# Decode attention, two blocks: the last output row in four column groups instead of two

## The chip, the cores and the metric

The kernel runs on one core of one Trainium2 chip. The metric is device time in microseconds for one execution, as the median of several runs. A profiled execution gives a trace beside it; its span is the time from the first to the last instruction, and lies about a microsecond below the measured time of a run.

## What is computed

Two independent attention blocks, A and B, each with one query token. A looks at the last 2048 positions of its key and value caches, B at all 8192. The two output rows of 576 values are concatenated.

```python
def block(x, k_cache, v_cache, wq, wo, W):        # A: W = 2048, B: W = 8192
    q = (x @ wq).reshape(1, 1, 32, 128).transpose(0, 2, 1, 3)
    k = jnp.repeat(k_cache[:, :, 8192 - W:, :], 2, axis=1)
    v = jnp.repeat(v_cache[:, :, 8192 - W:, :], 2, axis=1)
    p = softmax(jnp.einsum("bhqd,bhkd->bhqk", q, k) * 128 ** -0.5)
    o = jnp.einsum("bhqk,bhkd->bhqd", p, v)
    return o.transpose(0, 2, 1, 3).reshape(1, 1, 4096) @ wo      # wo: 4096 x 576
out = jnp.concatenate([block(A), block(B)], axis=-1)             # 1 x 1 x 1152, bf16
```

Everything is bf16. 102.76 MB are read from memory, nearly all of it the caches of 16 heads, wq and wo, each used once.

## The kernel before

The program is written as five lists of operations, one for each engine, in the order in which they are to run (`Prog`, L37). `op` adds an operation that tells the others by its engine's own semaphore; `load` adds one with a semaphore of its own (a DMA, or a copy whose end is counted with others). `deps` are names, which `emit` turns into waits. There is no scheduler: the order on each engine is the order in the source.

All loads are issued by SP in one order and go through a ring in SBUF of 72K bf16 values per partition (`place`, L167): wq of A and B, then K and V for units of four heads (four units of A, four of B), then wo of A in one piece and wo of B in five. `NWO` (L34) gives those pieces: A's 32 k at once, B's in 17, 8, 4, 2 and 1 k. One k is a slice of 128 rows of wo, 576 columns, spread over 128 partitions (147,456 bytes).

For each unit DVE transposes K in slabs (L350), PE makes scores (L367), ACT takes the exponent (L406), DVE transposes the probabilities, and PE multiplies by V (L431, four matmuls side by side in four strips of 32 columns of the array, each writing 32 partitions of a bank). The unit's result is copied out and folded (L438, L447). After the last unit the sums are inverted and the 32 heads' outputs are brought to the layout `oP`: partitions hold 128 rows of the contraction, and column k is the k-th slice (L482 to L499).

The output rows come last (L502 to L525). For each of the two blocks P and each k, two matmuls of one output row are made with `oP[:, P, k]` as weights: columns 0 to 319 (`N0` = 320) and columns 320 to 575. Both blocks use the bank `fb = qb[0]`. The four rows lie at partitions 0 and 32 (A) and 64 and 96 (B), that is, each in a strip of its own. The matmuls of one piece of wo are one operation, F*P.c*, that waits for that piece. F0.0 is A's, F1.0 to F1.4 are B's. When a block's last piece is done, ACT copies the 320 columns (L519) and DVE the 256 (L521) into one partition of `outsb`; both count on `s_row[P]`, and when it is 2, SP stores the row of 1152 bytes with one DMA (L523). SP's last operation waits until both stores have landed (`s_out` at 32).

Of the kernel before, what the change touches and what calls it, by code (L numbers as in the profile page):

```python
# [4 lines left out]
BF16 = mybir.dt.bfloat16  # L5
# [3 lines left out]
ACT = mybir.ActivationFunctionType  # L9
# [5 lines left out]
DM = 576  # L15
# [5 lines left out]
NQ = G // 4  # L21
# [6 lines left out]
ZA = 128 + 24  # L28
BIG = 1e30
N0 = 320  # L30
RING = 72 * 1024
NSEM = 24
NKT = 3
NWO = [[32], [17, 8, 4, 2, 1]]  # L34


class Prog:  # L37
# [9 lines left out]
    def op(self, eng, fn, deps=(), name=None):  # L47
        self.ops[eng].append((fn, tuple(deps), name, None))
        if name is not None:
            assert name not in self.where, name  # L50
            self.where[name] = (eng, len(self.ops[eng]) - 1)

    def load(self, eng, fn, sem, value, deps=(), name=None, step=16):
        self.ops[eng].append((fn, tuple(deps), None, (sem, step)))
        if name is not None:
            assert name not in self.dma, name
            self.dma[name] = (sem, value)
# [40 lines left out]
def bass_concat_heads__sliding_block_cached__gqa_block_cached__decode_kernel(nc, A_x, A_k_cache, A_v_cache, A_wq, A_wo,  # L98
# [6 lines left out]

    ring = nc.alloc_sbuf_tensor("ring", [128, RING], BF16)
    ktb = nc.alloc_sbuf_tensor("ktb", [128, NKT * SLAB], BF16)
# [35 lines left out]
    oq = nc.alloc_sbuf_tensor("oq", [128, 2, HQ], BF16)  # L143
    oP = nc.alloc_sbuf_tensor("oP", [128, 2, HQ], BF16)
    warm = nc.alloc_sbuf_tensor("warm", [128, 8], F32)
    outsb = nc.alloc_sbuf_tensor("outsb", [1, 2 * DM], BF16)

    sb = [nc.alloc_psum_tensor("sb%d" % b, [128, 512], F32) for b in range(2)]
    qb = [nc.alloc_psum_tensor("qb%d" % b, [128, 512], F32) for b in range(2)]
# [4 lines left out]
    def view(t, free, offset, dims, parts=128, p0=0):  # L154
        return bass.AP(tensor=t, offset=p0 * free + offset, ap=[[free, parts], *dims])

    pg = Prog(nc)
    op, load = pg.op, pg.load
    s_x = [nc.alloc_semaphore("s_x%d" % i) for i in range(2)]
    s_ld = [nc.alloc_semaphore("s_ld%d" % i) for i in range(NSEM)]  # L160
    s_out = nc.alloc_semaphore("s_out")
    s_row = [nc.alloc_semaphore("s_row%d" % i) for i in range(2)]
# [4 lines left out]
    def place(size, uses, issue, name):  # L167
        if at[0] + size > RING:
            at[0] = 0
        lo, hi = at[0], at[0] + size  # L170
        at[0] = hi
        deps = []
        for r in list(live):
            if r[0] < hi and lo < r[1]:
                deps += r[2]
                live.remove(r)
        n = nload[0]
        nload[0] += 1
        if n >= NSEM:
            deps += uses_of[n - NSEM]  # L180
        uses_of.append(list(uses))
        live.append((lo, hi, list(uses)))
        t = ring[:, lo:hi]
        load("sp", lambda e: issue(e, t), s_ld[n % NSEM], 16 * (n // NSEM + 1), deps=deps, name=name)
        return t
# [39 lines left out]
    for P in range(2):  # L225
        k0 = 0
# [6 lines left out]
    def slab(kind, i, s):  # L233
# [10 lines left out]
       deps=["id0"], name="ident")  # L244
# [15 lines left out]
    for c in range(2):  # L260
        op("dve", lambda e, c=c: e.tensor_reduce(par[:, c:c + 1], view(identf, 128, c, [[2, 64]]), AX.X, ALU.add),
           deps=["identf"], name="par%d" % c)
# [3 lines left out]
    for P in range(2):  # L266
        op("dve", lambda e, P=P: e.tensor_copy(  # L267
            view(xdup, 256, 128 * P, [[2, 64], [1, 2]], parts=1),
            view(xrow, 2 * DM, P * DM + 512, [[1, 64], [0, 2]], parts=1)), deps=["x%d" % P], name="xd%d" % P)
        for k in range(5):  # L270
            def mm(e, P=P, k=k):
                if k < 4:
                    lhsT = view(xrow, 2 * DM, P * DM + k, [[4, 128]], parts=1)
                else:
                    lhsT = xdup[0:1, P, :]
                return e.matmul(banks[2 * P + k // 4][:, (k % 4) * 128:(k % 4 + 1) * 128], lhsT=lhsT,  # L276
                                rhs=onesb[0:1, :], start=True, stop=True)
            op("pe", mm, deps=["x%d" % P, "onesb", "xd%d" % P], name="xT%d.%d" % (P, k))
        op("dve", lambda e, P=P: e.tensor_copy(
            xrep[:, P, 0:4, :].rearrange("p k m -> p (k m)"), banks[2 * P][:, :]), deps=["xT%d.3" % P], name="xr%d.0" % P)  # L280
        for c in range(2):
            op("dve", lambda e, P=P, c=c: e.tensor_scalar(
                xrep[:, P, 4 + c, :], banks[2 * P + 1][:, 0:128], par[:, c:c + 1], None, ALU.mult),
                deps=["xT%d.4" % P, "par%d" % c], name="xr%d.%d" % (P, 1 + c))
# [3 lines left out]
       deps=["identf"], name="clsb")  # L288
    op("dve", lambda e: e.tensor_reduce(clsa[:], view(identf, 128, 0, [[1, 8], [8, 16]]), AX.X, ALU.add),
       deps=["identf"], name="clsa")  # L290
    op("dve", lambda e: e.tensor_reduce(sel[:], view(identf, 128, 0, [[1, 32], [32, 4]]), AX.X, ALU.add),
       deps=["identf"], name="sel")
# [6 lines left out]
    for P in range(2):  # L299
        for n in range(8):  # L300
            u = 8 * P + n
            bank = banks[u % 4]

            def mm(e, P=P, n=n, bank=bank):
                for k in range(5):
                    if k < 4:
                        lhsT, o = xrep[:, P, k, :], wq_at[P, 0][:, k * w + n * 512:k * w + (n + 1) * 512]
                    else:
                        lhsT, o = xrep[:, P, 4 + n // 4, :], wq_at[P, 1][:, (n % 4) * 512:(n % 4 + 1) * 512]
                    ins = e.matmul(bank[:, :], lhsT=lhsT, rhs=o, start=(k == 0), stop=(k == 4))  # L310
                return ins
            op("pe", mm, deps=["wq%d.0" % P, "wq%d.1" % P] + XR + (["qe%d" % (u - 4)] if u >= 4 else []),
               name="qmm%d.%d" % (P, n))
            op("act", lambda e, u=u, bank=bank: e.activation(qsb[:, u % 4, :], bank[:, :], ACT.Copy),  # L314
               deps=["qmm%d.%d" % (P, n)] + (["qT%d" % (u // 2 - 2)] if u >= 4 else []), name="qe%d" % u)
            if n % 2:
                op("dve", lambda e, u=u, n=n: e.transpose(  # L317
                    ktb[:, (n - 1) * 512:(n + 1) * 512].bitcast(I32),
                    qsb[:, u % 4 - 1:u % 4 + 1, :].rearrange("p a n -> p (a n)").bitcast(I32)),
                    deps=["qe%d" % (u - 1), "qe%d" % u] + (["z0.%d" % i for i in range(4)] if P else []),  # L320
                    name="qT%d" % (u // 2))
        for b in range(4):
            if P == 1:
# [3 lines left out]
                    deps=["qT%d" % u for u in range(4, 8)] + ["zb0"], name="z1.%d" % b)  # L327
            else:
# [3 lines left out]
                    deps=["qT%d" % u for u in range(4)] + ["za0"], name="z0.%d" % b)  # L332
# [4 lines left out]
    k0 = [sum(nslab[:i]) for i in range(NU)]  # L337
# [117 lines left out]
    for i in range(NU):  # L455
        n = nslab[i + 1] if i + 1 < NU else 0
# [33 lines left out]
       deps=["lsel", "lselA", "nb%d" % last, "mr%d" % last], name="L")  # L490
# [3 lines left out]
        deps=["rl", "O%d" % last], name="on")  # L494
    op("dve", lambda e: e.transpose(oq[:].rearrange("p c k -> p (c k)"), on[:].rearrange("p c k -> p (c k)")),
       deps=["on"], name="oq")
# [2 lines left out]
    op("dve", lambda e: e.tensor_copy(oP[:].rearrange("p c k -> p (c k)"), mb[:, 64:128]), deps=["pm"], name="oP")  # L499


    fb = qb[0]  # L502
    for P in range(2):
        k0 = 0
        for c, kk in enumerate(NWO[P]):
            def mm(e, P=P, c=c, k0=k0, kk=kk):
                for k in range(kk):
                    for n in range(2):
                        r, lo, hi = 32 * (2 * P + n), n * N0, N0 + n * (DM - N0)
                        ins = e.matmul(fb[r:r + 1, 0:hi - lo], lhsT=oP[:, P, k0 + k:k0 + k + 1],  # L510
                                       rhs=wo_at[P, c][:, k * DM + lo:k * DM + hi],
                                       start=(k0 + k == 0), stop=(k0 + k == HQ - 1))
                return ins
            op("pe", mm, deps=["wo%d.%d" % (P, c), "oP", "exp%d" % (NQ - 2)], name="F%d.%d" % (P, c))
            k0 += kk
        done = "F%d.%d" % (P, len(NWO[P]) - 1)
        r, lo = 64 * P, P * DM

        load("act", lambda e, r=r, lo=lo: e.activation(outsb[0:1, lo:lo + N0], fb[r:r + 1, 0:N0], ACT.Copy),  # L519
             s_row[P], 2, deps=[done], name="f%d" % P, step=1)  # L520
        load("dve", lambda e, r=r, lo=lo: e.tensor_copy(outsb[0:1, lo + N0:lo + DM], fb[r + 32:r + 33, 0:DM - N0]),  # L521
             s_row[P], 2, deps=[done], step=1)
        load("sp", lambda e, lo=lo: e.dma_start(out[0, 0:1, lo:lo + DM], outsb[0:1, lo:lo + DM]),  # L523
             s_out, 16 * (P + 1), deps=["f%d" % P], name="out%d" % P)
    op("sp", None, deps=["out1"])  # L525

    pg.emit()
# [28 lines left out]
```

## Time and profile before

| | |
|---|---|
| time, median of 3 runs | 246.25 us (246.15 to 246.38) |
| profiled execution, span | 245.2 us |
| busy PE / DVE / ACT | 172.3 / 129.1 / 24.3 us |
| read from memory | 102.76 MB, 419 GB/s over the span |
| output matmuls (L510) | 128, busy 11.3 us, from 232.3 us on |
| weight loads of L510 | 128, 93 ns mean |
| copy of 320 columns (ACT L519) | 428 ns mean, two |
| copy of 256 columns (DVE L521) | 420 ns mean, two |
| stores (SP L523) | two of 1.1 KB, issued at 240.2 and 244.1 us |

Times in the trace are microseconds from the first instruction. Engines: PE is TensorE's matmul, PEld its weight load, which runs beside matmuls; DVE is VectorE, ACT ScalarE, SP the engine that issues the loads and stores here (its queue is SPq). A row of the timeline gives the start, the duration, what runs, its tiles (out<-in) with their shapes, and in brackets how long the engine had been idle and what ended that. The granted clock (PEclk) is the share of TensorE's full clock, in tenths in the 40 slices of the page and as a fraction in a table of stretches. The chain of waits goes back from the last instruction, at each step to what released it.

The page's DMA section counts, beside the kernel's loads, seven packets of 16 KB that carry instructions.

### The profile page before, as it was taken

How to read it: one execution, taken by the hardware profiler on the slowest of the kernel's cores; microseconds unless marked ns; L12 is line 12 of the kernel's file. 1: busy time of each engine (PE TensorE's matmuls, PEld its weight loads, DVE VectorE, ACT ScalarE, POOL GpSimd, SP SyncE). 2: the span in 40 equal slices, each digit the busy share in tenths (PEclk: the TensorE clock that was granted, in tenths of full speed). 3: DMA queues.
4: the chain of work that ended last, by engine and by line, in shares of the span. 5: the costliest groups of instructions: out<-in, count | busy, mean ns of one | idle time of the engine just before them, and what ended most of it. 6: DMA issues, size and time to landing. Idle time of an engine off the chain costs nothing.

```text
span 245.2 us, 2253 instructions
## 1 busy us (share of the span) xinstructions
PE 172.3 (70%) x960; PEld 71.8 (29%) x961; DVE 129.1 (53%) x162; ACT 24.3 (10%) x52; POOL 8.2 (3%) x15
## 2 busy tenths in 40 slices
PE   0269967787867994889582869945579939257197
PEld 0124422224433222432130523211423213213154
DVE  0422547667789986699501699810679920500201
ACT  2004540021201000100000100000010000200001
POOL 8400000000000000000000000000000000000000
PEclk9999995789999997569957578989657985677559
DMA  7999999999999999998999999999999999999994
GB/s 267 420 457 410 437 428 425 433 428 457 440 430 387 468 428 428 452 470 385 406 428 425 438 476 428 438 406 425 438 466 460 395 406 430 428 438 409 430 407 158
DMA packets 4481, 102.90 MB, mean 420 GB/s; under 512 B 500, under 2 KB 632, under 8 KB 1144
## 3 DMA queue, kind: packets, MB, share of 16 engines
q1 hardware_dynamic: 4468, 102.76, 97.9%
q8 instruction: 7, 0.11, 0.2%
q14 instruction: 2, 0.02, 0.0%
q10 hardware_dynamic: 4, 0.00, 0.0%
HBM read 102.76 MB, written 0.00 MB: 419 GB/s over the span
## 4 chain that ended last, share of the span: by engine, by line
DMA 55%; PE 29%; DVE 12%; ACT 2%; issue 2%; SPq 0%; DVEq 0%
DMA ring<-in_B_v_cache_dram 40%; DMA ring<-in_A_wo_dram 10%; DVE ktb L350 9%; PE vb L431 8%; DMA ring<-in_A_wq_dram 5%; PE qb L367 5%; PE qb L510 5%; PE sb L310 5%; PE qb L310 4%; ACT psb L406 1%; DVE pta L414 1%; PE ob L447 1%; PE sb L367 1%; PE qb L359 1%; PE mb L397 1%
## 5 line engine op out<-in xcount | busy, mean ns | idle before, releaser
L350 DVE STREAM_TRANSPOSE ktb<-ring 128x1024 int32<-128x1024 int32 x80 | 92.8, 1211 | 29.5 <-DMA ring<-in_B_k_cache_dram 28.3
L367 PE MATMUL sb<-ktb,zb 128*128 128x512 bf16 x256 | 76.0, 437 | 23.7 <-DVE ktb L350 21.1
L367 PEld LDWEIGHTS sb<-ktb,zb 128*128 128x128 bf16 x256 | 23.4, 106 | 72.4 <-DVE ktb L350 45.9
L431 PE MATMUL vb<-ring,pts 128*32 128x512 bf16 x256 | 24.7, 567 | 18.5 <-DMA ring<-in_B_v_cache_dram 14.4
L367 PE MATMUL qb<-ktb,za 128*128 128x512 bf16 x64 | 19.4, 449 | 2.8 <-DVE ktb L350 2.8
L431 PEld LDWEIGHTS vb<-ring,pts 128*32 128x32 bf16 x256 | 9.0, 134 | 33.6 <-DMA ring<-in_B_v_cache_dram 16.7
L438 ACT ACTIVATE xo<-vb 128x512 f32<-128x512 f32 x8 | 4.8, 597 | 129.4 <-PE vb L431 129.4
L418 DVE STREAM_TRANSPOSE pts<-psb 32x512 bf16<-32x512 bf16 x16 | 11.3, 703 | 9.5 <-ACT psb L406 9.3
L510 PE MATMUL qb<-ring,oP 128*1 128x256 bf16 (+1 forms) x128 | 11.3, 340 | 4.0 <-DMA ring<-in_A_wo_dram 4.0
L317 DVE STREAM_TRANSPOSE ktb<-qsb 128x512 int32<-128x512 int32 x8 | 5.7, 711 | 15.0 <-ACT qsb L314 15.0
L310 PE MATMUL sb<-ring,xrep 128*128 128x512 bf16 x40 | 11.4, 442 | 2.7 <-DMA ring<-in_A_wq_dram 2.7
L447 PEld LDWEIGHTS ob<-sel,xo 128*128 128x128 f32 x64 | 10.9, 244 | 3.8 <-ACT xo L438 2.2
L447 PE MATMUL ob<-sel,xo 128*128 128x8 f32 x64 | 10.1, 285 | 1.2 <-ACT xo L438 1.2
L367 PEld LDWEIGHTS qb<-ktb,za 128*128 128x128 bf16 x64 | 6.1, 109 | 13.4 <-issue 5.8
L310 PE MATMUL qb<-ring,xrep 128*128 128x512 bf16 x39 | 9.5, 393 | 0.0
L510 PEld LDWEIGHTS qb<-ring,oP 128*1 128x1 bf16 x128 | 7.0, 93 | 8.3 <-DMA ring<-in_A_wo_dram 4.1
L521 DVE CAST outsb<-qb 1x256 bf16<-1x256 f32 x2 | 0.8, 420 | 14.7 <-PE qb L510 14.7
L491 DVE RECIPROCAL rl<-mb 128x64 f32<-128x64 f32 x1 | 0.6, 558 | 12.3 <-PE mb L488 12.3
L276 PE MATMUL sb<-onesb,xrow 1*128 1x128 bf16 x4 | 0.6, 298 | 9.2 <-DVE xdup L267 9.2
L392 DVE TENSOR_REDUCE mr<-mb 1x8 f32<-1x128 f32 x8 | 1.9, 240 | 9.5 <-PE mb L384 9.5
L310 PEld LDWEIGHTS sb<-ring,xrep 128*128 128x128 bf16 x40 | 4.3, 109 | 8.6 <-issue 5.3
L314 ACT ACTIVATE qsb<-sb 128x512 bf16<-128x512 f32 x8 | 4.8, 597 | 19.1 <-PE sb L310 19.1
(65 smaller groups left out, 68.8 us busy)
## 6 DMA issues: line engine op xcount, KB each, us to landing
ring<-in_B_k_cache_dram SPq DMA_DIRECT2D x8, 4096.0 KB, 24.5
ring<-in_A_k_cache_dram SPq DMA_DIRECT2D x4, 2048.0 KB, 30.5
ring<-in_A_v_cache_dram SPq DMA_DIRECT2D x4, 2048.0 KB, 25.4
ring<-in_B_v_cache_dram SPq DMA_DIRECT2D x2, 4096.0 KB, 23.8
ring<-in_A_wo_dram SPq DMA_DIRECT2D x1, 4608.0 KB, 23.9
ring<-in_A_wq_dram SPq DMA_DIRECT2D x1, 4096.0 KB, 12.5
ring<-in_B_wq_dram SPq DMA_DIRECT2D x1, 4096.0 KB, 22.6
ring<-in_B_wo_dram SPq DMA_DIRECT2D x1, 2448.0 KB, 29.3
```

Of the source, the lines that this page charges most:

```text
L310: ins = e.matmul(bank[:, :], lhsT=lhsT, rhs=o, start=(k == 0), stop=(k == 4))
L314: op("act", lambda e, u=u, bank=bank: e.activation(qsb[:, u % 4, :], bank[:, :], ACT.Copy), deps=["qmm%d.%d" % (P, n)] + (["qT%d" % (u // ...
L317: op("dve", lambda e, u=u, n=n: e.transpose(ktb[:, (n - 1) * 512:(n + 1) * 512].bitcast(I32), qsb[:, u % 4 - 1:u % 4 + 1, :].rearrange("p ...
L350: op("dve", lambda e: e.transpose(kt.bitcast(I32), src.bitcast(I32)), deps=[landed] + (["S%d" % (k - NKT)] if k >= NKT else Z), name="T%d. ...
L359: e.matmul(bank[:, :], lhsT=mkl[:].rearrange("p a h r -> p (a h r)"), rhs=mkr[:].rearrange("p q h -> p (q h)"), start=True, stop=False)
L367: ins = e.matmul(bank[:, :], lhsT=lhsT, rhs=view(ktb, KT, (k % NKT) * SLAB + 64 * c + v, [[128, 16], [2, 32]]), start=(side == "B" and s = ...
L397: op("pe", lambda e: e.matmul(mb[:, 128:129], lhsT=mexp[0:1, :], rhs=onesf[0:1, 0:1], start=True, stop=True), deps=["mx%d" % i, "ones"], n ...
L418: op("dve", lambda e, b=b: e.transpose(view(pts, NB * 128, 2 * b, [[8, 16], [128, NB], [1, 2]], 32, 32 * b), psb[32 * b:32 * b + 32, :]), ...
L431: ins = e.matmul(vbank[i][32 * j:32 * j + 32, :], lhsT=lhsT, rhs=src[:, 512 * j:512 * j + 512], start=(s == 0), stop=(s == nslab[i] - 1))
L438: op("act", lambda e: e.activation(xo[:, c, :], vbank[i][:, :], ACT.Copy), deps=["V%d.%d" % (i, nslab[i] - 1)] + (["O%d" % (i - 1)] if i e ...
L447: ins = e.matmul(ob[:, at:at + 8], lhsT=xo[:, c, 128 * t:128 * t + 128], rhs=sel[:, 8 * t:8 * t + 8], start=(t == 0), stop=(t == 3))
L510: ins = e.matmul(fb[r:r + 1, 0:hi - lo], lhsT=oP[:, P, k0 + k:k0 + k + 1], rhs=wo_at[P, c][:, k * DM + lo:k * DM + hi], start=(k0 + k == 0 ...
```

## The change

A's row stays as it is: two column groups in `qb[0]`, copied into partition 0 of `outsb`, stored in one piece. B's row is computed in the other bank, `qb[1]`, in four groups of 144 columns at partitions 0, 32, 64 and 96. ACT copies partitions 0 to 32 (33 of them, of which the first and the last carry results) and DVE partitions 64 to 96, 144 columns each, into a new tile `outq` at the same partitions. One DMA stores four pieces of 288 bytes, from partitions 0, 32, 64 and 96. B's matmuls name the exponent of A's last unit (exp3) as a dependency, in place of exp2, since `qb[1]` held that unit's scores. The pieces of wo and their loads are unchanged.

```diff
+N1 = DM // 4
...
-    outsb = nc.alloc_sbuf_tensor("outsb", [1, 2 * DM], BF16)
+    outsb = nc.alloc_sbuf_tensor("outsb", [1, DM], BF16)
+    outq = nc.alloc_sbuf_tensor("outq", [128, N1], BF16)
...
-    fb = qb[0]
+    parts = [[(0, 0, N0), (32, N0, DM)], [(32 * j, N1 * j, N1 * j + N1) for j in range(4)]]
     for P in range(2):
-        k0 = 0
+        fb, k0 = qb[P], 0
         for c, kk in enumerate(NWO[P]):
-            def mm(e, P=P, c=c, k0=k0, kk=kk):
+            def mm(e, P=P, c=c, k0=k0, kk=kk, fb=fb):
                 for k in range(kk):
-                    for n in range(2):
-                        r, lo, hi = 32 * (2 * P + n), n * N0, N0 + n * (DM - N0)
+                    for r, lo, hi in parts[P]:
                         ins = e.matmul(fb[r:r + 1, 0:hi - lo], lhsT=oP[:, P, k0 + k:k0 + k + 1],
                                        rhs=wo_at[P, c][:, k * DM + lo:k * DM + hi],
                                        start=(k0 + k == 0), stop=(k0 + k == HQ - 1))
                 return ins
-            op("pe", mm, deps=["wo%d.%d" % (P, c), "oP", "exp%d" % (NQ - 2)], name="F%d.%d" % (P, c))
+            op("pe", mm, deps=["wo%d.%d" % (P, c), "oP", "exp%d" % (NQ - 2 + P)], name="F%d.%d" % (P, c))
             k0 += kk
...
+        else:
+            load("act", lambda e: e.activation(outq[0:33, :], qb[1][0:33, 0:N1], ACT.Copy),
+                 s_row[P], 2, deps=done, name="f1", step=1)
+            load("dve", lambda e: e.tensor_copy(outq[64:97, :], qb[1][64:97, 0:N1]), s_row[P], 2, deps=done, step=1)
+            load("sp", lambda e: e.dma_start(
+                bass.AP(tensor=out.tensor, offset=out.offset + DM, ap=[[N1, 4], [1, N1]]),
+                bass.AP(tensor=outq, offset=0, ap=[[32 * N1, 4], [1, N1]])), s_out, 32, deps=["f1"], name="out1")
```

In the kernel after, the matmuls of both rows stand at line 511.

More of the change, by code (lines that the diff above doesn't have):

```diff
@@ L513, in mm @@
                 return ins
-            op("pe", mm, deps=["wo%d.%d" % (P, c), "oP", "exp%d" % (NQ - 2)], name="F%d.%d" % (P, c))
+            op("pe", mm, deps=["wo%d.%d" % (P, c), "oP", "exp%d" % (NQ - 2 + P)], name="F%d.%d" % (P, c))
             k0 += kk
[L516 to L524, printed above, removed]
+        done = ["F%d.%d" % (P, len(NWO[P]) - 1)]
+        if P == 0:
+            load("act", lambda e: e.activation(outsb[0:1, 0:N0], qb[0][0:1, 0:N0], ACT.Copy),
+                 s_row[P], 2, deps=done, name="f0", step=1)
+            load("dve", lambda e: e.tensor_copy(outsb[0:1, N0:DM], qb[0][32:33, 0:DM - N0]),
+                 s_row[P], 2, deps=done, step=1)
+            load("sp", lambda e: e.dma_start(out[0, 0:1, 0:DM], outsb[0:1, :]), s_out, 16, deps=["f0"], name="out0")
+        else:
[5 more added lines that the diff above has]
+                bass.AP(tensor=outq, offset=0, ap=[[32 * N1, 4], [1, N1]])), s_out, 32, deps=["f1"], name="out1")
     op("sp", None, deps=["out1"])
```

## The prediction

> **What bounds the kernel now.** First the page's slices: how busy the DMA engines are, and the clock that TensorE was granted.
>
> ```profile
> span 245.2 us, 2253 instructions
> ...
> PEclk9999995789999997569957578989657985677559
> DMA  7999999999999999998999999999999999999994
> ```
>
> The DMA engines are at 90% or more in nearly every slice but the last, so the end is set by when the last bytes of weights land, and by what follows them. Then the chain of waits, from 220 us on.
>
> ```profile
> 5 pieces in order of time: start us, us, what
> 208.37 23.91 DMA ring<-in_A_wo_dram
> 232.28 0.04 issue
> 232.32 11.31 PE qb L510 x94
> 243.63 0.02 issue
> 243.65 0.43 ACT outsb L519
> ```
>
> The chain names the output matmuls of L510 for 11.31 us, but it stops at the copy, and a chain of PE work doesn't say whether PE was waiting. The timeline of the last stretch does.
>
> ```profile
> 242.96 0.09 PEld L510 LDWEIGHTS qb<-ring,oP 128*1 128x1 bf16 x4 [0.21 <-DMA ring<-in_B_wo_dram]
> 243.31 0.08 PEld L510 LDWEIGHTS qb<-ring,oP 128*1 128x1 bf16 x2 [0.26 <-DMA ring<-in_B_wo_dram]
> 243.65 0.43 ACT L519 ACTIVATE outsb<-qb 1x320 bf16<-1x320 f32 x1 [3.47 <-PE qb L510]
> 243.65 0.43 DVE L521 CAST outsb<-qb 1x256 bf16<-1x256 f32 x1 [3.49 <-PE qb L510]
> 244.11 0.25 SPq L523 DMA_DIRECT2D out_dram<-outsb  x1
> ```
>
> The last two pieces of B's wo (F1.3, F1.4) are waited for: the weight loads stood idle 0.21 and 0.26 us for a DMA. By the trace's landings the last piece was complete at 243.27; matmuls began at 243.31 and ended at 243.61, the copies ran 243.65 to 244.08, the store was issued at 244.11, its landing counted at 245.22, and SP passed its wait at 245.23. These links, 0.04 + 0.30 + 0.04 + 0.43 + 0.03 + 1.12, are the tail of 1.96 us behind the last landing, and the change can shorten or lengthen only that, unless it makes PE late. How near PE is to late is read from stretches of PE work and clock.
>
> ```profile
> core 0: us, PE busy (x) PEld busy (x) DVE busy (x) ACT busy (x) POOL busy (x), PEclk, DMA share, GB/s
> ...
> 232.32:238.21 5.89, 5.89 (x49) 3.48 (x50) 0.00 (x0) 0.00 (x0) 0.00 (x0) 0.50 0.97 412
> 238.21:241.63 3.42, 3.42 (x62) 2.46 (x60) 0.41 (x1) 0.43 (x1) 0.00 (x0) 1.00 0.88 357
> 241.63:245.20 3.57, 1.98 (x25) 1.01 (x22) 0.43 (x1) 0.43 (x1) 0.00 (x0) 1.00 0.10 37
> ```
>
> A's row ran at half clock until 238.21. In the trace's matmul starts, one k (a 320 and a 256 column matmul in two strips, side by side) takes 267 ns at half clock and 136 ns at full clock. F1.2's last k ended about 242.95, and F1.3 had landed at 242.92: PE is late by a hair there, and DMA sets F1.4.
>
> **The change part by part.** The sum is made against the profiled 245.2 us; the runs' median, 246.25, lies 1.05 above it, which I carry over.
>
> *Matmuls of B's row.* Each k becomes four matmuls of 144 columns in four strips. A 320 column matmul lasts 297 to 299 ns and a 256 column one 270 to 273, so 64 columns are 27 ns and 144 columns about 223 ns. In the last piece four start instead of two; neighbours in different strips start 3 to 4 ns apart (so at 243.31, and in the V matmuls at 214.4). The last begins about 12 ns behind the first and ends at 0.235 instead of 0.30: -0.06 us. The pieces before it have cover: 144 columns in a strip are 136 x 144/320 = 61 ns per k, so F1.0's 17 k need 1.0 us instead of 2.3 and PE waits for every landing. The other bound is that four pairs of weight load and matmul can't be issued in 61 ns; that is the second rival. I take cover, as the trace shows eight matmuls and weight loads start within 12 ns at 214.4.
>
> *Another bank, the wait on exp3 instead of exp2.* exp3 (L406, the fourth unit) ended at 75.2 us; F1 also no longer shares a bank with A's copies. Strips 0 and 32 are busy with F0 until 239.54, so F1.0 starts up to 0.5 us later there, inside the slack of F1.0 (1.0 us of work before 240.83, when F1.1 lands). Nothing.
>
> *More instructions.* 64 more weight loads and 64 more matmuls. The trace has seven 16 KB instruction packets, at about each 256 PE instructions (191, 479, 699, 950, 1232, 1481, 1752 started); PE has 1941 now and 2069 then, so an eighth falls near 241 us. In the landings of successive loads each such packet sets one DMA engine back by some 1.5 us for good, each time another one. At the last piece the engines post at 240.92 to 241.72 (eight not set back), up to 242.88 (seven), and 243.27 (one). A fresh engine set back 1.5 us ends by 243.2: nothing, hidden by the straggler. If it hits a late one: 242.88 + 1.5, or +1.1 us.
>
> *Copies.* Partitions cost nothing: DVE's casts from PSUM, 128x64 at 224 ns and 128x512 at 692, make a line (1.04 ns a column) on which the 1x256 copy should take 425, and it took 420. So 33x144 on DVE is 224 + 80 x 1.04 = 307 ns. ACT: 428 at 1x320 and 597 at 128x512, 0.88 ns a column, gives 273; from 171 at 128x1 it is 290. The later of the two counts: 0.31 instead of 0.43, -0.12 us.
>
> *The store.* One piece of 1152 bytes becomes four of 288, from four partitions. No row shows it. Nearest below: the one piece store, issue 0.25 us, its packet starting 0.72 after the issue; as its packet took 54 ns, four side by side could save 0.04 at most. Nearest above: the first weight load of 128 pieces over 16 engines, issue 0.41, its first packet 1.03 after the issue and the last engine's 1.31, so +0.31 to +0.59. Four pieces are nearer to one than to 128; taking about a sixth of 0.59, +0.10 us, with ends of -0.04 and +0.59. The Trainium skill (DMA: Bandwidth & Descriptors, Specifications) says that transfers below 512 B make the DMA engine read, modify and write. By it pieces of 288 B are dearer than the 1152 B row; it gives no time, and no run here shows a store so small.
>
> *Sum.* -0.06 - 0.12 + 0.10 = -0.08 us: span 245.1, time **246.17**. Its own range by the ends of the store and 0.02 on the copies: 246.25 - 0.24 = 246.01 to 246.25 + 0.43 = 246.68.
>
> **The rivals.**
>
> *PE was the bound in the timed runs.* The clock changes in steps of 3.41 us, whose phase against the kernel need not be fixed. It rose at 238.21 here; the step before, from 231.39, held 0.93 us without work and didn't raise it. With the phase up to 0.93 later (beyond that, the earlier step is full of work too) up to half of that, 0.46, would be added to the old PE chain, and the new one at 61 ns a k would take it all back: 246.17 - 0.46 = 245.71. For it: PE's hair of lateness at F1.2. Against: the three runs lie within 0.23 us.
>
> *Issue becomes the bound, the other side.* 128 matmuls with as many weight loads in place of 64. In the densest stretch of the trace 64 matmuls start in 3.84 us, 60 ns each. If that were the pace at which PE is fed, F1's last would start at 239.01 + 128 x 0.060 = 246.69 and end 0.22 later, 3.30 later than now; with the copies and the store 246.25 + 3.28 = 249.5. It decides from 34 ns per matmul on (124 matmuls in the 4.26 us from 239.01 to 243.27). Strips that don't overlap would do the same (576 columns, 245 ns a k). Against: that stretch is full of strips busy with 320 and 256 columns, so its 60 ns need no other cause; 16 matmuls started 42 ns apart around 239, and L431's V matmuls run at 54 ns, which is 512 columns in four strips. The Trainium skill (TensorE: Matmul & The Clock Gate, "Wait — 56ns, not 53.3ns?") names about 62 ns per matmul where microcode decodes it, and a floor of 25 ns otherwise. By the first F1 takes 128 x 62 = 7.9 us; by the second 3.2 us, an estimate from that page, which is under the present 4.3.
>
> *The short pieces are read before they are written.* A read's price is that of the 1152 byte loads of x: from data packet to completion packet 1.26 us, where a store shows 0.05. +1.2 in the store's path: 246.17 + 1.2 = 247.4. It is slower by over 0.2% once the store costs 0.67 more than one piece. For it: nothing in the trace, which has no such store. Against: a write's landing here came 0.33 us behind its packet, and a merge at the memory may hide in that.
>
> *The eighth instruction packet hits a late engine:* 246.17 + 1.1 = 247.3. Against: all before it hit fresh ones.
>
> **How the numbers follow.** 0.2% (0.49 us) is about what a measurement of this kernel can tell from no change. Forecast 0.64, PE bound in the timed runs 0.10, issue 0.09, read before write 0.12, late engine 0.04, other 0.01. Faster: 0.10 and a tail of the forecast, 0.12. Slower: 0.09 + 0.12 + 0.04 and a tail, 0.26. Within: 0.62. The range runs from 245.65, under the first rival, to 247.2, over the forecast's end and into the third; left out are issue, about half of the third and the fourth.
>
> **What would show it.** L511's matmuls in four strips, 61 ns a k at full clock, and every piece of B's wo waited for, F1.1 for about half a microsecond. Copies of 0.28 and 0.31 us. The store's issue to its landing at 1.1 to 1.3 us; 2 us or more is read before write. Were the last weight loads not idle before their piece, issue or strips bind. Were the last landing later than the store's shares explain, look for a late engine. A store's piece cost over 0.67, or a pace over 34 ns, makes the forecast wrong.

## The result, and the profile after

| | before | after |
|---|---|---|
| time, median of 18 runs each | 246.33 us | 246.72 us (246.62 to 247.0) |
| profiled span | 245.2 us | 245.4 us |
| last piece of wo landed | 243.27 us | 242.99 us |
| from that landing to the end of the span | 1.98 us | 2.38 us |

The changed kernel is slower: ratio 1.0018, 95% interval 1.0012 to 1.0024, that is 0.30 to 0.59 us. The spans differ by less than that because the last loads happened to land 0.28 us earlier in the profiled execution of after; in the four profiles of kernels with two groups (before and three runs below) that landing lies anywhere between 242.92 and 243.27 us. What the change can touch is the tail behind that landing, and it grew by 0.39 us, as much as the medians differ.

The timeline of after, from 240 us on (start, duration, what, and the idle time before it):

```profile
240.57 0.47 PEld L511 LDWEIGHTS qb<-ring,oP 128*1 128x1 bf16 x32 [1.06 <-DMA ring<-in_B_wo_dram]
240.57 0.67 PE L511 MATMUL qb<-ring,oP 128*1 128x144 bf16 x32 [0.86 <-DMA ring<-in_B_wo_dram]
241.94 0.22 PEld L511 LDWEIGHTS qb<-ring,oP 128*1 128x1 bf16 x16 [0.90 <-DMA ring<-in_B_wo_dram]
...
243.03 0.09 PEld L511 LDWEIGHTS qb<-ring,oP 128*1 128x1 bf16 x4 [0.24 <-DMA ring<-in_B_wo_dram]
243.31 0.28 ACT L525 ACTIVATE outq<-qb 33x144 bf16<-33x144 f32 x1 [4.20 <-PE qb L511]
243.32 0.31 DVE L527 CAST outq<-qb 33x144 bf16<-33x144 f32 x1 [4.21 <-PE qb L511]
243.65 0.63 SPq L528 DMA_DIRECT2D out_dram<-outq  x1
```

Below, the issue of a store is the time that the engine's queue spends on its instruction, and the landing is when its last share is counted at the semaphore, both reckoned from the start of the issue. The reader is to see three things. The 32 matmuls of F1.1 (8 k in four strips) take 0.67 us from first start to last end, and PE then waits for every piece. The copies take 0.28 and 0.31 us. And the last line, the issue of the store, takes 0.63 us where it took 0.25. By the trace's landings the store's last share is counted 1.68 us behind its issue, where one piece took 1.11. The loss lies ahead of the data: the first packet starts 1.25 us behind the issue in place of 0.72, and from there to the landing it is 0.42 us in place of 0.39.

The chain of waits of after now begins with the last pieces of wo, no longer with A's:

```profile
209.34 33.65 DMA ring<-in_B_wo_dram
242.99 0.04 issue
243.03 0.26 PE qb L511 x4
243.29 0.02 issue
243.32 0.31 DVE outq L527
```

The tail link by link, from the landing of F1.4 to the start of the store's issue: 0.04 + 0.23 + 0.05 + 0.31 + 0.03, which is 0.67 us before rounding, against 0.84 before (the chain above draws the line between matmuls and copy 0.03 us later); from the issue to the end of the span 1.71 against 1.14.

### The profile page after: what moved, and what is told of

It reads as the page before. It is cut to its first block, busy times and chain, and to the rows that moved or that the text cites. A ratio compares the mean times of both kernels' runs of the same rounds, so it can differ in the third digit from the quotient of the medians.

```text
span 245.4 us, 2382 instructions
## 1 busy us (share of the span) xinstructions
PE 170.1 (69%) x1025; PEld 72.1 (29%) x1025; DVE 128.9 (53%) x162; ACT 24.1 (10%) x52; POOL 8.1 (3%) x15
## 4 chain that ended last, share of the span: by engine, by line
DMA 70%; PE 17%; DVE 9%; issue 1%; SPq 1%; ACT 1%; DVEq 0%
DMA ring<-in_B_v_cache_dram 39%; DMA ring<-in_B_wo_dram 14%; DMA ring<-in_B_k_cache_dram 12%; DVE ktb L352 8%; PE vb L433 7%; DMA ring<-in_A_wq_dram 5%; PE sb L312 4%; PE qb L312 4%; PE sb L369 1%; SPq L231 1%; PE ob L449 1%; ACT psb L408 0%; DVE ktb L319 0%; DVE pta L416 0%; DVE zb L326 0%
## 5 line engine op out<-in xcount | busy, mean ns | idle before, releaser
L433 PE MATMUL vb<-ring,pts 128*32 128x512 bf16 x256 | 23.5, 544 | 20.5 <-DMA ring<-in_B_v_cache_dram 16.4
L449 PEld LDWEIGHTS ob<-sel,xo 128*128 128x128 f32 x64 | 12.6, 279 | 4.0 <-ACT xo L440 2.4
L511 PE MATMUL qb<-ring,oP 128*1 128x144 bf16 (+2 forms) x192 | 9.3, 273 | 4.7 <-DMA ring<-in_A_wo_dram 2.8
L449 PE MATMUL ob<-sel,xo 128*128 128x8 f32 x64 | 11.7, 311 | 1.2 <-ACT xo L440 1.2
L511 PEld LDWEIGHTS qb<-ring,oP 128*1 128x1 bf16 x192 | 5.9, 87 | 8.1 <-DMA ring<-in_A_wo_dram 2.9
L405 ACT ACTIVATE nb<-mb 128x1 f32<-128x1 f32 x8 | 1.4, 171 | 48.0 <-PE mb L399 48.0
```

The source lines that it names most:

```text
L433: ins = e.matmul(vbank[i][32 * j:32 * j + 32, :], lhsT=lhsT, rhs=src[:, 512 * j:512 * j + 512], start=(s == 0), stop=(s == nslab[i] - 1))
L449: ins = e.matmul(ob[:, at:at + 8], lhsT=xo[:, c, 128 * t:128 * t + 128], rhs=sel[:, 8 * t:8 * t + 8], start=(t == 0), stop=(t == 3))
```

## The experiments

The first experiments asked whether the store alone explains the loss, and by what it is dear. All ratios are to runs of the kernel before on the same chip.

**One piece in after**, from the tile of A's row, so that B's row comes out with A's values and only the form of the store is asked.

```diff
-                bass.AP(tensor=out.tensor, offset=out.offset + DM, ap=[[N1, 4], [1, N1]]),
-                bass.AP(tensor=outq, offset=0, ap=[[32 * N1, 4], [1, N1]])), s_out, 32, deps=["f1"], name="out1")
+            load("sp", lambda e: e.dma_start(out[0, 0:1, DM:2 * DM], outsb[0:1, :]), s_out, 32, deps=["f1"], name="out1")
```

> The kernel after, but B's row is stored as one piece of 1152 bytes from one partition (it holds A's row, so B's values are not those of the reference); matmuls and copies as in after. Store theory (all that was lost is the store of four pieces, 0.57 us from issue to landing, and matmuls and copies gave 0.18): 0.15 to 0.2 us under the kernel before, store's issue 0.25 us and landing 1.1 us behind it. Rival (the instruction page more, the bank or the 64 further matmuls cost something too): not under the kernel before.

Measured: 246.19 us against 246.33 (0.9994, 0.9985 to 1.0003); issue 0.25 us, landing 1.10 behind it. The median is 0.14 below, a little less than the 0.15 to 0.20 expected, and the interval reaches over zero; but against after's 246.72 half a microsecond is gone with the store's form alone. The eighth instruction packet, the other bank and the added matmuls are all still in this kernel, so they cost nothing that shows.

**Pieces from one partition in before** (n = 4, 2, 16; the source steps one column less than a piece, so that they stay separate pieces).

```diff
-        load("sp", lambda e, lo=lo: e.dma_start(out[0, 0:1, lo:lo + DM], outsb[0:1, lo:lo + DM]),
+        m = n if P else 1
+        load("sp", lambda e, lo=lo, m=m: e.dma_start(
+            bass.AP(tensor=out.tensor, offset=out.offset + lo, ap=[[DM // m, m], [1, DM // m]]),
+            bass.AP(tensor=outsb, offset=lo, ap=[[2 * DM, 1], [DM // m - (m > 1), m], [1, DM // m]])),
```

> The kernel before, with B's row stored as four pieces of 288 bytes from one partition (the pieces are 143 columns apart in the source, so that they stay pieces; B's values are shifted by up to three columns). Pieces theory (each piece or DMA engine more costs, wherever it comes from): issue near 0.63 us, landing near 1.68 behind the issue, 0.5 to 0.6 us over the kernel before. Partition theory (four source partitions cost): issue 0.25 to 0.3, within 0.1 us of the kernel before. Read-before-write theory (short pieces land late): issue unchanged, landing late behind the packets.

> The same with two pieces of 576 bytes. If the cost goes by the piece (0.57 for three more, 0.19 each): 0.15 to 0.2 us over the kernel before. If any store of several pieces pays one step (another path for a second dimension, or the write of the rest of the count for the engines not used): 0.4 to 0.6 us over. If pieces under 512 bytes are what costs: 0 to 0.1 over.

> The same with sixteen pieces of 72 bytes. By the piece: 15 x 0.19 = 2.8 us over the kernel before. One step for any store of several pieces: 0.4 to 0.7 over. If the step is the write of the rest of the count (16 less the engines used), which sixteen pieces don't need: issue 0.3 to 0.45 as with loads of 128 pieces, 0.1 to 0.3 over.

Measured, against 246.33: four pieces 247.07 us (1.0035, 1.0021 to 1.0049; 0.74 over, where 0.5 to 0.6 was expected), two 246.90 (1.0024, 1.0015 to 1.0033), sixteen 246.94 (1.0028, 1.0018 to 1.0038). From the timeline with two pieces, the issue:

```profile
243.76 0.71 SPq L524 DMA_DIRECT2D out_dram<-outsb  x1
```

and from the one with four:

```profile
244.00 0.73 SPq L524 DMA_DIRECT2D out_dram<-outsb  x1
```

Two pieces (0.71 us issue, 1.73 to the landing) cost as much as sixteen (0.61 and 1.76). So it is not a price by the piece, and not pieces under 512 bytes (two pieces have 576). It looked then like one step for any store of several pieces. That reading fell later.

**Is it a first time?** Both rows in four groups and four pieces, so that the same form is issued twice (all places where P told the rows apart use `parts[0]` = `parts[1]`, `outq[P]`).

> The kernel after with A's row treated as B's: four groups, four pieces, so that SP issues a store of this form 4 us before the last one. Cold theory (the step of some 0.4 us in the issue and 0.6 to the landing is paid by the first DMA of this form, as ACT's first load of x took 0.50 us and its second 0.21): the first store's issue near 0.63 us, the second near 0.3, time 0.1 to 0.2 us under the kernel before. Path theory (every store of several pieces pays it): both issues near 0.63 us, time as after, 0.35 to 0.45 us over the kernel before.

Measured: 246.62 us against 246.34 (1.0012, 1.0003 to 1.0021). The first store's issue took 0.65 us, the second's 0.56, and its landing came 1.60 behind; the time is 0.28 over the kernel before, where the path theory had 0.35 to 0.45. A first time costs 0.09 us at most, and the first store of one piece in before took 0.07 longer than the second, too; the rest is the form's own.

**Stores of one piece, several of them.** DVE's copy goes to partitions 0 and 32 beside ACT's (groups ordered 0, 2, 1, 3 over the strips), and the two halves are stored separately, by SP and ACT, or both by SP; or after's four pieces are four stores, two on each queue.

```diff
...
+            load("dve", lambda e: e.tensor_copy(outq[0:33, N1:2 * N1], qb[1][64:97, 0:N1]), s_row[P], 2, deps=done,
+                 step=1)
+            load("sp", lambda e: e.dma_start(out[0, 0:1, DM:DM + 2 * N1], outq[0:1, :]), s_out, 48, deps=["f1"],
+                 name="out1")
+            load("act", lambda e: e.dma_start(out[0, 0:1, DM + 2 * N1:2 * DM], outq[32:33, :]), s_out, 48, deps=["f1"])
```

> B's row in four groups; DVE writes its two groups to partitions 0 and 32 beside ACT's, so that two partitions hold 288 columns each; two stores of one piece (576 bytes) each, one issued by SP, one by ACT. If the step belongs to a DMA of several pieces alone: both issues 0.25 us (ACT's up to 0.5, if its first after a long time is slow), time 0.05 to 0.2 us under the kernel before. If a second store costs by itself (its descriptors or its landing wait behind the first): 0 to 0.3 us over the kernel before.

> As with two queues, but SP issues both stores of one piece. The second is issued 0.27 us behind the first: 0.18 gained, 0.27 lost, 0.05 to 0.15 us over the kernel before, 0.27 slower than with two queues if ACT's issue is as fast as SP's.

> The kernel after with four stores of one piece (288 bytes), two issued by SP and two by ACT. Each issue 0.25 us, the second of each queue 0.27 later than the first: 0.18 gained, 0.27 lost, 0.05 to 0.15 us over the kernel before, if short pieces cost nothing by themselves. If pieces under 512 bytes land later (read before written): the landings over 1.3 us behind their issue, 0.3 us and more over the kernel before.

Measured, against 246.34: two queues 246.35 us (1.0001, 0.9992 to 1.0011), both on SP 246.51 (1.0008, 1.0000 to 1.0017; 0.16 behind two queues, where 0.27 was expected), four stores 246.62 (1.0013, 1.0004 to 1.0022). The timeline with two queues:

```profile
243.30 0.28 ACT L525 ACTIVATE outq<-qb 33x144 bf16<-33x144 f32 x1 [4.32 <-PE qb L511]
243.30 0.31 DVE L527 CAST outq<-qb 33x144 bf16<-33x144 f32 x1 [4.33 <-PE qb L511]
243.64 0.25 SPq L529 DMA_DIRECT2D out_dram<-outq  x1
243.64 0.23 ACTq L531 DMA_DIRECT2D out_dram<-outq  x1
```

Both issues are short and start together, and the data packets start at 244.35 and 244.39. But the landings are counted at 244.72 and 244.90, 0.18 us apart. With four stores they come at 244.66, 244.84, 245.02 and 245.20, again 0.18 apart, though the packets had all gone by 244.72. So the second store cost what the copies gained. With both on SP the packets start at 244.36 and 244.65 and the landings come as far apart, at 244.73 and 245.02. Four stores were expected 0.05 to 0.15 over the kernel before and came out 0.28 over; in the trace the last landing comes 1.32 us behind the issue of the last store, in place of 1.11. The pieces of 288 bytes are not slow by themselves, as four adjacent ones below show.

**Sixteen and eight pieces from adjacent partitions** (0 to 15, or 0 to 7, of `outq`; the diff for sixteen). Most of these partitions hold no result, so B's row comes out with other values here and in the next two runs; they ask for the time of the store alone.

```diff
-                bass.AP(tensor=out.tensor, offset=out.offset + DM, ap=[[N1, 4], [1, N1]]),
-                bass.AP(tensor=outq, offset=0, ap=[[32 * N1, 4], [1, N1]])), s_out, 32, deps=["f1"], name="out1")
+                bass.AP(tensor=out.tensor, offset=out.offset + DM, ap=[[DM // 16, 16], [1, DM // 16]]),
+                bass.AP(tensor=outq, offset=0, ap=[[N1, 16], [1, DM // 16]])), s_out, 32, deps=["f1"], name="out1")
```

> The kernel after, but the store takes sixteen pieces of 72 bytes from partitions 0 to 15 (B's values are not those of the reference). If the step is the same for every store of several pieces: issue 0.55 to 0.65 us, landing 1.65 to 1.8 behind it, time as after. If it is the search for a number of engines below sixteen, or the write of the rest of the count: issue 0.33 to 0.45, as for loads of 128 pieces from 128 partitions, 0.2 us under after.

> The kernel after, with a store of eight pieces of 144 bytes from partitions 0 to 7 (B's values are not those of the reference). If only a store that uses all sixteen engines is issued fast (0.34 us with sixteen partitions, 0.63 with four): issue 0.55 us or more and landing 1.6 or more behind it. If the issue gets dearer by each engine fewer (0.29 more for twelve fewer): about 0.44, landing 1.45. If four partitions 32 apart were what cost: 0.34, landing 1.3.

Measured: sixteen 246.35 us against 246.36 (1.0004, 0.9995 to 1.0012), issue 0.34, landing 1.32; eight 246.21 against 246.25 (0.9994, 0.9985 to 1.0003), issue 0.30, landing 1.19. So a store of several pieces need not be dear, and pieces of 72 bytes land as soon after their packets (1.15 to 1.32 behind the issue, first packet at 0.83) as one of 1152 (1.11, 0.72). "Only with all sixteen engines" was wrong too: eight were cheaper still.

**Four adjacent partitions, and eight that are apart.** This separates the number of pieces from the step between their partitions. The diff is that for four; in the one for eight the step is `4 * N1` and the pieces are as in the run with eight adjacent ones.

```diff
...
-                bass.AP(tensor=outq, offset=0, ap=[[32 * N1, 4], [1, N1]])), s_out, 32, deps=["f1"], name="out1")
+                bass.AP(tensor=outq, offset=0, ap=[[1 * N1, 4], [1, DM // 4]])), s_out, 32, deps=["f1"], name="out1")
```

> The kernel after, with the same four pieces of 288 bytes taken from partitions 0 to 3 instead of 0, 32, 64 and 96 (B's values are not those of the reference). Step theory (a source whose partitions are not adjacent is dear): issue 0.25 to 0.3 us, landing 1.1 to 1.2 behind it, 0.1 to 0.15 us under the kernel before, 0.5 under after. Count theory (four pieces are dear, eight and sixteen aren't): issue near 0.63, landing near 1.68, time as after.

> The kernel after, with eight pieces of 144 bytes from partitions 0, 4, 8 to 28 (B's values are not those of the reference). Step theory: issue near 0.6 us, landing near 1.65 behind it, time as after. Count theory: 0.30 and 1.19, as with eight adjacent partitions. If only a step of 32 partitions is dear: as with adjacent ones.

From the timeline with four pieces from partitions 0 to 3:

```profile
243.09 0.09 PEld L511 LDWEIGHTS qb<-ring,oP 128*1 128x1 bf16 x4 [0.24 <-DMA ring<-in_B_wo_dram]
...
243.71 0.27 SPq L528 DMA_DIRECT2D out_dram<-outq  x1
```

and with eight from partitions 0, 4, 8 to 28:

```profile
243.26 0.31 DVE L527 CAST outq<-qb 33x144 bf16<-33x144 f32 x1 [4.39 <-PE qb L511]
243.60 0.77 SPq L528 DMA_DIRECT2D out_dram<-outq  x1
```

The same four pieces of 288 bytes are issued in 0.27 us in place of 0.63 and land at 1.17 in place of 1.68 when their partitions are adjacent: 246.24 us against 246.27 (0.9996, 0.9987 to 1.0005), half a microsecond under after. The 0.1 to 0.15 us under the kernel before that were expected don't show in the times; in the trace the tail behind the last landing is 1.87 us in place of 1.98. Eight with a step of 4 partitions take 0.77 and 1.81: 246.92 (1.0023, 1.0014 to 1.0032). The cause is settled by two pairs in which only the step between partitions differs, four pieces here and in after, and eight here and above:

| source of the store | issue, us | last landing behind the issue, us |
|---|---|---|
| one piece | 0.25 | 1.11 |
| 4 / 8 / 16 adjacent partitions | 0.27 / 0.30 / 0.34 | 1.17 / 1.19 / 1.32 |
| 4 partitions, step 32 (after) | 0.63 | 1.68 |
| the same, as the second store of its form (both rows) | 0.56 | 1.60 |
| 8 partitions, step 4 | 0.77 | 1.81 |
| 2 / 4 / 16 pieces within one partition | 0.71 / 0.73 / 0.61 | 1.73 / 1.78 / 1.76 |

Dear is a source whose pieces don't lie one to a partition in a row. Only the steps of 32 (four pieces) and 4 (eight) were run, and whether pieces within one partition, whose pattern has a dimension more, are dear for the same reason isn't shown. Nor does the trace show what SP does in the additional 0.35 to 0.5 us of issue.

**Four copies into one partition.** This keeps the short matmuls and the cheap store (ACT and DVE copy two groups each, 1x144, to partition 0).

> B's row in four groups as in after, but each engine copies its two groups of 144 columns one after the other into one partition, and one DMA stores one piece. Copies 0.28 + 0.28 on ACT and 0.31 + 0.31 on DVE if they don't overlap: 0.2 longer than the 0.43 of before, matmuls 0.06 shorter: 0.1 to 0.15 us over the kernel before. If the second copy starts before the first has ended (a copy's fixed part hidden): 0.45 to 0.5, within 0.05 us of the kernel before.

The timeline:

```profile
243.16 0.59 ACT L528 ACTIVATE outq<-qb 1x144 bf16<-1x144 f32 x2 [4.93 <-PE qb L511]
243.16 0.64 DVE L531 CAST outq<-qb 1x144 bf16<-1x144 f32 x2 [4.95 <-PE qb L511]
243.83 0.25 SPq L532 DMA_DIRECT2D out_dram<-outq  x1
```

246.65 us against 246.25 (1.0015, 1.0006 to 1.0024). The second copy starts only when the first has ended (0.59 and 0.64 for two), 0.21 us longer than before's 0.43. That explains half of the measured 0.40, which is over the 0.10 to 0.15 expected: the spans of these runs are 0.2 us longer than those of the kernel before (medians 245.1 and 244.9), and the other 0.2 lies between span and measured time, where no trace shows its cause.

**PE kept busy.** In seven profiles of kernels with B's row in four groups the clock had fallen to half when the last piece's matmuls ran (with two queues 0.01 us after their start), and they ended 0.33 us behind the landing in place of 0.28. For the kernel with two queues, the table of busy time by stretches, cut at the clock's step:

```profile
core 0: us, PE busy (x) PEld busy (x) DVE busy (x) ACT busy (x) POOL busy (x), PEclk, DMA share, GB/s
...
239.56:242.97 3.41, 1.41 (x61) 0.81 (x60) 0.00 (x0) 0.00 (x0) 0.00 (x0) 1.00 0.63 244
242.97:244.90 1.93, 0.28 (x4) 0.07 (x4) 0.31 (x1) 0.28 (x1) 0.00 (x0) 0.50 0.00 1
```

PE was busy 1.41 us of the step that ended at 242.97, and the next one runs at half clock. Six matmuls were added to that kernel where PE waits:

```diff
+            if P and c < 2:
+                op("pe", lambda e: [e.matmul(vb[0][:, :], lhsT=perm[:, :], rhs=wo_at[1, 0][:, 512 * i:512 * i + 512],
+                                             start=True, stop=True) for i in range(3)][-1])
```

> The kernel with two stores on two queues, and after F1.0 and after F1.1 three matmuls of 128x512 more into a bank that is no longer used (their result is not read), while PE would wait for the next piece. Clock theory (the last matmuls ran at half clock there, ending 0.33 us behind the last landing in place of 0.28, because PE stood idle too long before them): full clock to the end, 0.28, and 0.05 us less time than without the fillers, at most 0.1. If the clock at the end doesn't hang on PE's work: half clock, and no gain.

246.37 us against 246.36 (1.0000, 0.9991 to 1.0009). In its profile the clock stayed full and the matmuls ended at 0.28, but the steps fell at 240.5 and 243.9 there, so that a fall could only have come after them. Four other profiles with B's row in four groups, after's among them, had that luck without fillers, so this run settles nothing about the time, and an effect of 0.05 us lies under what the times resolve. On the clock it says a little more: no fall followed the step that ended at 243.9, in which PE was busy for 2.51 us. In the ten profiles with B's row alone in four groups and no fillers, PE was busy for 1.21 to 1.62 us of the step that ended 6.8 us after the clock had risen, and each time half clock followed. So PE's idle time is a likely cause of the fall, but busy time alone doesn't decide it: in the trace of before, PE was busy for 2.42 us from 207.48 to 210.91 us, and half clock followed there, too.

No version was found that is faster than the kernel before beyond its interval. The best with B's whole row, two queues, is equal to it; the store from adjacent partitions, which by its trace would leave a gain of 0.1 us that its times don't resolve, needs the four results in adjacent partitions, which the copies used here don't give.

## Why the prediction was wrong

The forecast was 0.08 us faster; measured is 0.39 slower. The time lies within the range, but the sign is wrong, and one term of the sum made it so.

- **The store** was the step that failed: "Four pieces are nearer to one than to 128; taking about a sixth of 0.59, +0.10 us". It cost 1.68 - 1.11 = +0.57, close to the upper end of +0.59. That the end from the load of 128 pieces held is luck: the issue alone, 0.63 us, is longer than that load's 0.41, and eight pieces that lie apart cost 0.70. The way between the ends was taken by the number of pieces, and the runs show that the number hardly counts (0.06 us for four adjacent pieces) and that the partitions' step does. The prediction had named "from four partitions" and given it no price. With 0.57 in place of 0.10 its sum is -0.06 - 0.12 + 0.57 = +0.39, the measured difference. The sign turned as soon as the store cost more than 0.18, so the sixth that was taken decided it. Of the signs that the prediction named, 1.1 to 1.3 us to the landing for the forecast and 2 us or more for read before write, the measured 1.68 is neither.
- **The copies** were right: 307 ns forecast for DVE and 310 measured; 273 to 290 for ACT and 283 measured. That 33 partitions cost no more than one is shown (copies of 1x144 took 0.28 us on ACT and 0.30 to 0.31 on DVE).
- **The matmuls** were right where the clock stayed full: 223 ns each, done 0.23 us after the first start. Not foreseen: in seven of the profiles with four groups, where PE waits longer, the clock had fallen by then, and only 0.01 of the 0.06 us was left. In the four profiles of kernels with two groups this didn't happen; that the waits bring it isn't shown.
- **Cover of the pieces before** was right: 62 ns a k (61 forecast), and the weight loads wait 0.24 to 1.06 us for each of F1.1 to F1.4. For F1.0 there was no wait: it had landed at 237.80, before A's row was done. F1.1's wait is 1.06 us and not about half a microsecond, as in this execution the clock had risen 1.8 us earlier (236.37 in place of 238.21) and A's row was copied 1.1 us sooner.
- **Issue becomes the bound** is refuted: 32 matmuls with their weight loads go out at 16 ns each, under every pace that the prediction weighed.
- **PE was the bound in the timed runs**: no sign of it; the one-piece version gained 0.14, and not up to 0.46 more.
- **Read before write** is refuted as a price that shows: pieces of 72 bytes landed within 0.5 us of their packets. The Trainium skill (DMA: Bandwidth & Descriptors, Specifications) has transfers below 512 B read, modified and written; whether that happens the trace can't tell, but it took no time that a store of this size shows.
- **The eighth instruction packet** came, at 241.66 us, and the last landing was not later for it (242.99). The times of the one-piece version, which has it too, say the same.

## What to carry to other kernels

At the end of a kernel the store's issue and landing are on the path in full, and the form of its source can outweigh the engines' work before it: here 0.5 us between adjacent partitions and partitions with a step. When an edit scatters a small result over partitions to shorten matmuls and copies, price the gathering by a run of that one store, not by the count of its pieces. A faster engine in front of a wait also idles longer, and on PE the lower clock then came in seven of eleven profiles before or with the work that counts; whether the idling brings it is open.

## What the runs showed of the hardware

- The issue of the last store on SP took 0.25 us for one piece, 0.27 to 0.34 for 4 to 16 adjacent partitions, and 0.56 to 0.77 where the pieces were apart or within one partition; first packets and landings moved with it (0.72 us and 1.11 for one piece, 1.25 and 1.68 in after).
- Stores of one piece that two queues sent together were counted as landed 0.18 us apart (two stores: 244.72 and 244.90; four: 244.66, 244.84, 245.02, 245.20), while the shares of one store of four pieces came 0.01 us apart, the last 0.05. Two stores from one queue, whose packets started 0.29 us apart, landed 0.29 apart.
- Two copies out of one bank on the same engine don't overlap: 0.28 and 0.31 us each, 0.59 and 0.64 for two.
- TensorE's clock fell to half 6.8 us after it had risen wherever A's row had two groups and B's four, without fillers: at the end of a step of 3.41 us in which PE was busy for 1.21 to 1.62 us (1.41 with two queues, 1.55 in after). With six fillers PE was busy 2.51 us of the step, and it didn't fall; with two groups for both it stayed full to the end of the matmuls.
